# VectorE's share of a softmax exponential: the closing sum made of 16-bit tiles, a second GpSimd pass, and a new port rule and pace table in the instruction plan

## The chip, the cores and the metric

One core of one Trainium2 chip runs the whole program. The core has TensorE (PE in the profile; its weight loads are PEld), VectorE (DVE), ScalarE (ACT), GpSimd (POOL) and SyncE (SP), which here issues the DMAs. The metric is the device time of one execution in microseconds; the kernel before took 835.02 us (median of 3 runs, 834.14 to 835.98).

## The reference

```
x = x + A(layernorm(x)); x = x + B(layernorm(x))      # twice, same weights
A: qkv = x @ wqkv; 16 heads of 28; p = softmax(q k^T * 28**-0.5); (p v) @ wo
B: relu(x @ w1 + b1)**2 @ w2 + b2
```

x has 2048 rows of 448 in bf16, B's hidden width is 1792. In each of the two layers the softmax takes the exponential of 16 x 2048 x 2048 scores; the rest is matrix products, two layernorms and a squared relu.

## The kernel before, in words

The scores of one layer are cut into units. A unit is 128 keys by 512 columns, as two or four key blocks of one head against 256 or 128 queries. There are 2048 units in the two layers. TensorE writes three units into one group of PSUM banks (`s_stream`, matmuls at L956); one ScalarE instruction takes the exponential of a whole group, 128 x 1536 (L986 in `e_stream`), and writes bf16 into a tile `pt`. TensorE then multiplies by the values (L1127 in `p_stream`).

Some units are taken from ScalarE and given to VectorE and GpSimd. Then the group's ScalarE instruction is 128 x 1024 wide, and the third unit is worked by four instructions (`a_unit` and `a_rest`), on scores that are already multiplied by 128 times log2(e):

- the **take**, VectorE, L1034: from PSUM into a 32-bit tile w (`v_w`, or spare room in `K_sb`), score plus a shift, held from below. The shift is such that the low 16 bits of the 32-bit float hold the fraction of the power of two;
- the **part**, GpSimd, L1051: the low 16 bits of w (read as uint16, every second one), minus a middle, times a factor, to a bf16 tile (`pt`'s third bank, `pd`, or spare room in `V_sb` and `h`);
- the **bend**, VectorE, L1057: that bf16 tile squared in place;
- the **close**, VectorE, L1064: one scalar-tensor-tensor, w plus a constant plus the bend, rounded to int16. Its 16 bits are the bf16 exponential.

The order of every instruction of every engine is written out when the program is built. A planner (`Planner.run`) keeps a clock per engine, takes an estimated duration for each piece of work (`Op`), and at each step issues the candidate that could start first, then the one of smaller priority number. Pieces with `port=True` are planned so that one of GpSimd and one of VectorE do not overlap: the later one is planned from the end of the other. All units are handed out in that run: `apart` gives a unit to VectorE only if a set w is free, if VectorE was not more than 99.5% planned in the last 11 us, and if its backlog (the planned clock less now, plus `left`, the estimate of work that opened units still owe) is not above an entry of the table PACE, which has 128 entries over the run. The order is fixed on the chip; what moves is only when the semaphores let an instruction go.

Around the exponentials the planner puts everything else: the projections (L686 with evictions L705, L709, L737), layernorm (L528, L533, L649 on VectorE, L555 and L556 on GpSimd), output sums (L1154, L1156), the normalisation by DMA through DRAM (L1231, L1236, L1242, L1250, L1255), the hidden layer (L1322, and the square L1331) and the residual sums (L1264). Before a group of scores, TensorE repeats its score matmuls when the plan has it idle there (`again`).

Of the kernel before, what the change touches and what calls it, by code (L numbers as in the profile page):

```python
# [11 lines left out]
DT = mybir.dt  # L12
AF = mybir.ActivationFunctionType
ALU = mybir.AluOpType
# [9 lines left out]


FRAC = 7
GY = 0.617
XL = 0.25
TICK = 1.8
# [1 line left out]
WARM2 = 0.55  # L31
SHARE = 0.9
YL = 0.05
GN = 0.718
GM = 1.275
GS = 1.3
# [8 lines left out]
EXP_BITS = (127.0 - 0.085177) * 128 - EXP_SHIFT  # L45
# [37 lines left out]
LEAD = 15  # L83
LAST = 690
BUSY = 0.995
PACE = (2.2, 2.2, 2.2, 2.2, 1.8, 2.2, 2.2, 1.4, 3.0, 1.4, 1.4, 1.4, 2.2, 3.2, 3.6, 2.2, 2.2, 2.2, 2.2, 2.2, 0.6, 3.4, 2.6, 1.8, 1.0, 1.8, 2.6, 2.6, 2.2, 3.8, 3.0, 2.2, 2.2, 3.6, 2.2, 0.6, 3.0, 1.8, 1.8, 1.8, 1.8, 2.6, 2.2, 2.2, 1.4, 3.4, 2.6, 1.0, 2.2, 3.4, 3.6, 3.6, 1.4, 2.2, 3.0, 2.6, 3.8, 3.4, 1.8, 1.0, 2.6, 2.6, 2.2, 2.2, 3.8, 3.0, 1.8, 1.0, 3.8, 3.0, 1.8, 2.2, 2.2, 1.4, 3.2, 4.4, 2.6, 3.6, 3.6, 1.4, 1.8, 3.6, 3.0, 3.0, 3.0, 3.0, 2.2, 2.2, 2.2, 2.2, 3.0, 3.0, 1.8, 2.2, 2.6, 2.6, 1.4, 1.4, 4.0, 3.6, 3.6, 1.8, 1.8, 2.2, 2.2, 3.6, 1.4, 1.4, 2.2, 4.0, 1.8, 1.4, 2.2, 1.8, 2.6, 2.6, 2.2, 2.2, 2.6, 2.2, 2.8, 3.2, 1.4, 1.8, 1.8, 2.2, 2.2, 2.2)
SPAN = 11
NPT = 11
NOS = 2
# [58 lines left out]
class Planner:  # L148
# [61 lines left out]
    def run(self):  # L210
        while self.streams:
            cands = []
            for st in self.streams:
                s, e = self.earliest(st[2]) if st[2] is not None else (None, None)
                if s is not None:
                    cands.append((s, st[0](s) if callable(st[0]) else st[0], e, st))
            assert cands, "no stream can go on"
            known = cands

            due = next((c[3][2].ready for c in cands if c[1] == 0), None)  # L220
            if due is None:
                due = next((c[0] + c[3][2].dur + LAT["ACT"] for c in cands if c[1] == 1), None)
            if due is not None:
                ok = [c for c in cands if c[2] != "PE" or c[1] == 0 or c[0] + c[3][2].dur <= due + self.slack()]
                cands = ok or cands
            s, _, e, st = min(cands, key=lambda c: (max(c[3][2].ready, self.clock[c[2]]) if c[2] == "PE" and self.turns() else c[0], c[1]))
            o = st[2]
            o.eng = (e,)
            if o.acq:
                o.res = min((r for r in (o.acq() if callable(o.acq) else o.acq) if r.when() is not None), key=lambda r: r.when())  # L230
                o.turn = len(o.res.rel)
                o.res.rel.append(None)
            o.start, o.end = s, s + o.dur
            if e == "PE":
                o.room = min([c[0] for c in known if c[2] == "PE" and c[3] is not st] or [1e9]) - o.end
            if o.fn:
                o.fn(e)
            o.end += o.more
            self.clock[e] = o.end - (OVER if e == "DVE" and o.dur > 0.1 else 0.0)
            if e == "PE":  # L240
                self.mode = o.mode
            if o.port and e in self.ports:
                self.ports[e] = [*self.ports[e][-5:], (s, o.end)]
            if e == "PE" and o.end > s:
                self.used = [u for u in self.used if u[1] > s - 2 * TICK] + [(s, o.end, SHARE * o.dur if o.w is None else o.w)]
            if e in self.past:
                self.past[e] = [p for p in self.past[e] if p[1] > s - 40.0] + [(s, max(s, self.clock[e]))]
            for a in o.rel:
                a.got.append(o.end + o.lat + LAT[e])
                if len(a.got) == a.need:  # L250
                    a.res.rel[a.turn] = max(a.got)
            for key in o.sets:
                self.tok[key] = o
            st[2] = next(st[1], None)
            if st[2] is None:
                self.streams.remove(st)
# [3 lines left out]
def kernel(  # L260
# [12 lines left out]
    nc = tc.nc  # L273
    _, S, D = A_x.shape
# [6 lines left out]

    q_scale = float(DH) ** -0.5 * float(np.log2(np.e)) * 2.0 ** FRAC

# [255 lines left out]
    def layernorm(t0, nt, deps_of, early=False, mv=None, place=None, x_in=None, parts=False):  # L539
# [95 lines left out]
        for p0 in range(0, nt, wide):  # L635
# [4 lines left out]
            for j in js:  # L640
# [11 lines left out]
                on = NORMG and not early  # L652
                nm = Op("POOL" if on else "DVE", GN if on else 0.39, norm, deps=[rss[j], *([] if x_in is None else [x_in])], sets=[("n", t0, j)] if early else (), port=True)
                yield nm
# [181 lines left out]
    left = [0.0]  # L836

    def sets_of(unit):

        pi, kb, r, hh = unit  # L840
        l, qb, *_ = passes[pi]
        if l == 0:
            return R_v if 2 <= qb <= 6 else R_v[:4]
        return R_v

    def apart(i, now, us, soon=SOON):
# [22 lines left out]
        if pl.load(SPAN, "DVE") > BUSY:  # L869
            return None  # L870
        if max(0.0, pl.clock["DVE"] - now) + left[0] > PACE[i * len(PACE) // len(units)]:
            return None
# [93 lines left out]
    def apart_from(gi, t):  # L966

        if "read" in gbuf[gi]:
            tc.declare_no_dep(t.ins, gbuf[gi]["read"].ins, reason="both read the scores, in banks of their own")
        gbuf[gi]["read"] = t  # L970

    def e_stream():
        gi = 0
        while gi < len(gbuf) or s_left:
# [8 lines left out]
            def fn(e, gi=gi, n=n):  # L983
                e_now[:] = [e_now[0] + n // 512 + ("x" in gbuf[gi]), gi]
                pt = gbuf[gi]["pt"]
                t = nc.scalar.activation(out=pt[:, 0:n], in_=gbuf[gi]["sc"][:, 0:n], func=AF.Exp,  # L986
                                         scale=float(np.log(2.0)) * 2.0 ** -FRAC)
                if gbuf[gi].get("x") is gbuf[gi]["s"]:
# [17 lines left out]
    def pd_of(o):  # L1006
        i = R_pd.index(o.res)
        if i == 0:
            return vp.tile([P, 512], DT.bfloat16, name="pd")[:, :]
        if i < 5:  # L1010
            return V_sb[1][:, 11 + i, :, :].rearrange("p h r -> p (h r)")
        if i > 5:
            return V_sb[0][:, 8 + i, :, :].rearrange("p h r -> p (h r)")
        return hp.tile([P, QB], DT.bfloat16, name="h")[:, :]

    v_w = [const.tile([P, 512], DT.float32, name=f"v_w{k}") for k in range(4)]
    two = lambda a: a.rearrange("p (a n) -> p a n", a=2)

    def set_of(res, l):

        k = R_v.index(res)
        if k < 4:
            return two(v_w[k][:, :])
        keys = K_sb[1 - l][:, :, S - 512:S] if l == 0 else K_sb[0][:, :, 0:512]
        return keys[:, 2 * k - 8:2 * k - 6, :].bitcast(DT.float32)

    def a_unit(gi, x, src, unit, l):
        yield Op("-", 0.0, None, deps=[("s", gi)])
        box = {}

        def take(e):
            pending[0] -= 1
            box["w"] = set_of(c.res, l)
            t = nc.vector.tensor_scalar(out=box["w"], in0=two(src), scalar1=EXP_SHIFT,  # L1034
                                        scalar2=EXP_LOW, op0=ALU.add, op1=ALU.max)
            if x is gbuf[gi]["s"]:
                apart_from(gi, t)
        c = Op("DVE", 0.69, take, deps=[("s", gi)], acq=sets_of(unit), rel=x)
        left[0] += 1.54
        yield c  # L1040
        left[0] -= 0.6
        pl.spawn(lambda now: V_LAST if e_now[1] - gi >= V_AGE or at[0] > ends_at[unit[0]] + V_PAST else V_LATE if now > c.end + V_WAIT else V_PRIO if gi > FIRST else V_FIRST, a_rest(gi, c, box, unit))

    def a_rest(gi, c, box, unit):

        own = gbuf[gi]["in"]

        def part(e):
            pd = gbuf[gi]["pd"] = gbuf[gi]["pt"][:, 1024:1536] if own else pd_of(y)
            low = box["w"].bitcast(DT.uint16).rearrange("p a (n t) -> p a n t", t=2)[:, :, :, 0]  # L1050
            nc.gpsimd.tensor_scalar(out=two(pd), in0=low, scalar1=-EXP_MID * 65536, scalar2=EXP_BEND, op0=ALU.add, op1=ALU.mult)  # L1051
        y = Op("POOL", GY, part, deps=[c, ("p", gi)] if own else [c], acq=None if own else lambda: pd_free(unit), port=True, lat=YL)
        yield y

        def bend(e):
            pd = gbuf[gi]["pd"]
            nc.vector.tensor_tensor(out=pd, in0=pd, in1=pd, op=ALU.mult)  # L1057
        h = Op("DVE", 0.42, bend, deps=[y], port=True)
        yield h
        left[0] -= 0.34  # L1060

        def close(e):
            pd = gbuf[gi]["pd"]
            nc.vector.scalar_tensor_tensor(out=two(pd.bitcast(DT.int16)), in0=box["w"], scalar=EXP_BITS, in1=two(pd),  # L1064
                                           op0=ALU.add, op1=ALU.add)
        o = Op("DVE", 0.683, close, deps=[h], rel=c, sets=("x", gi), port=True, lat=XL)
        gbuf[gi]["x"] = y
        yield o
        left[0] -= 0.6

    norm_done = {}
    rows_done = set()
# [531 lines left out]
```

## Time and profile before

| | before |
|---|---|
| median of 3 runs | 835.02 us |
| span of the profiled execution | 834.4 us |
| instructions in it | 26688 |
| ScalarE busy | 815.2 us |
| VectorE busy | 793.5 us |
| TensorE busy (modelled) | 780.0 us |
| GpSimd busy | 234.8 us |
| units on VectorE (takes, L1034) | 272 |

The span runs from the first to the last instruction; here it is 0.6 us below the median of the runs. Busy is the union of an engine's instruction records, so time in which an instruction's record is open but waits inside for a port counts as busy. Records of neighbouring VectorE instructions overlap a little, so the spacing of two starts is what one costs, and not its own length.

### The profile page before, as it was taken

What the parts mean: (1) busy time and instruction counts of PE and PEld (TensorE: products, weight loads), DVE (VectorE), ACT (ScalarE), POOL (GpSimd) and SP (SyncE); (2) the same over time, 40 slices, a digit from 0 to 9 for tenths busy, and PEclk for the clock granted to TensorE, in tenths of its full rate; (3) what the DMA queues carried; (4) which work ended last, traced back from release to release, by engine and by line L of the source; (5) the groups of instructions that cost most, each with busy time, mean ns of one, the idle gap of its engine ahead of it and who ended that gap; (6) DMA issues with size and microseconds to landing.
All of it is one profiled execution on the core that took longest, in us unless ns stands there. A gap on an engine that the chain in (4) does not pass through costs nothing.

```text
span 834.4 us, 26688 instructions
## 1 busy us (share of the span) xinstructions
PE 780.0 (93%) x11403; PEld 405.6 (49%) x11403; DVE 793.5 (95%) x1646; ACT 815.2 (98%) x700; POOL 234.8 (28%) x366
## 2 busy tenths in 40 slices
PE   8999889999999999998999999989999999999997
PEld 4445545554444455444444544435454544545565
DVE  7999999999999999999999999999999999999955
ACT  8999999999999999999999999999999999999993
POOL 3222232233223232322223223332223132242200
PEclk9999999999999999999999999699999999999999
DMA  9200100000000000000000000011000000000000
GB/s 247 75 2 3 28 16 15 15 15 16 15 3 14 15 15 16 15 5 12 2 2 2 2 2 3 16 29 29 24 18 20 20 26 21 21 16 12 21 14 13
DMA packets 32359, 17.88 MB, mean 21 GB/s; under 512 B 17833, under 2 KB 31787, under 8 KB 32240
## 3 DMA queue, kind: packets, MB, share of 16 engines
q1 hardware_dynamic: 32240, 16.18, 7.0%
q8 instruction: 89, 1.46, 0.7%
q14 instruction: 30, 0.25, 0.1%
HBM read 13.88 MB, written 2.07 MB: 19 GB/s over the span
## 4 chain that ended last, share of the span: by engine, by line
DVE 40%; ACT 26%; PE 25%; issue 8%; DMA 0%; POOL 0%; ACTq 0%; DVEq 0%
ACT pt L986 26%; PE mt L686 10%; PE sc L956 8%; DVE v_w L1034 6%; DVE pt L1064 5%; PE oT L1127 4%; DVE r L1322 4%; DVE pt L1057 3%; DVE K_sb L1034 3%; DVE V_sb L1064 2%; DVE x_sb L1264 2%; DVE V_sb L1331 1%; DVE h L1064 1%; DVE V_sb L1057 1%; DVE xn L649 1%
## 5 line engine op out<-in xcount | busy, mean ns | idle before, releaser
L986 ACT ACTIVATE pt<-sc 128x1536 bf16<-128x1536 f32 (+1 forms) x683 | 803.8, 1407 | 4.3 <-PE sc L956 3.3
L956 PE MATMUL sc<-Q_sb,K_sb 32*128 32x256 bf16 (+1 forms) x4412 | 278.4, 267 | 36.0 <-ACT pt L986 28.6
L956 PEld LDWEIGHTS <-K_sb 32*128 32x128 bf16 x4412 | 106.6, 92 | 213.3 <-issue 154.7
L1127 PE MATMUL oT<-pt,V_sb 128*32 128x256 bf16 (+1 forms) x4004 | 154.8, 270 | 1.1 <-DVE K_sb L596 0.4
L1034 DVE TENSOR_SCALAR v_w<-sc 128x512 f32<-128x512 f32 x194 | 131.2, 681 | 4.1 <-PE sc L956 3.3
L686 PE MATMUL mt<-xnT,w 128*128 128x256 bf16 (+1 forms) x872 | 116.4, 272 | 3.6 <-DVE r L1322 0.9
L1127 PEld LDWEIGHTS <-V_sb 128*32 128x32 bf16 x4352 | 91.8, 96 | 53.8 <-issue 47.9
L1051 POOL TENSOR_SCALAR pt<-v_w 128x512 bf16<-128x512 uint16 x85 | 61.4, 723 | 158.6 <-DVE v_w L1034 138.5
L686 PEld LDWEIGHTS <-w 128*128 128x128 bf16 x896 | 75.8, 98 | 37.2 <-issue 28.2
L1322 DVE TENSOR_SCALAR r<-mt 128x512 bf16<-128x512 f32 x107 | 72.5, 680 | 2.6 <-PE mt L686 2.3
L1051 POOL TENSOR_SCALAR V_sb<-v_w 128x512 bf16<-128x512 uint16 x54 | 39.2, 726 | 101.6 <-DVE v_w L1034 101.4
L686 PE MATMUL mt<-w,V_sb 128*128 128x448 bf16 x260 | 66.9, 355 | 0.0
L1064 DVE SCALAR_TENSOR_TENSOR pt<-v_w,pt 128x512 int16<-128x512 f32 x85 | 57.2, 680 | 0.0
L1034 DVE TENSOR_SCALAR K_sb<-sc 128x512 f32<-128x512 f32 x78 | 52.9, 680 | 2.4 <-PE sc L956 1.9
L1057 DVE TENSOR_TENSOR pt<-pt 128x512 bf16<-128x512 bf16 x109 | 49.1, 463 | 0.0
L1264 DVE TENSOR_TENSOR x_sb<-x_sb,mt 128x448 bf16<-128x448 bf16 x61 | 37.1, 609 | 5.5 <-PE mt L686 5.3
L1057 DVE TENSOR_TENSOR V_sb<-V_sb 128x512 bf16<-128x512 bf16 x89 | 40.1, 460 | 0.0
L528 DVE BATCH_NORM_STATS2 st<-x_sb 128x6 f32<-128x448 bf16 x63 | 38.6, 614 | 1.6 <-DMA x_sb<-in_A_x_dram 1.2
L1051 POOL TENSOR_SCALAR V_sb<-K_sb 128x512 bf16<-128x512 uint16 x35 | 24.6, 703 | 51.7 <-DVE K_sb L1034 44.3
L1064 DVE SCALAR_TENSOR_TENSOR V_sb<-v_w,V_sb 128x512 int16<-128x512 f32 x54 | 37.5, 694 | 0.1
L686 PEld LDWEIGHTS <-V_sb 128*128 128x128 bf16 x302 | 24.5, 98 | 25.7 <-issue 12.6
L1051 POOL TENSOR_SCALAR h<-v_w 128x512 bf16<-128x512 uint16 x29 | 20.5, 708 | 45.1 <-DVE v_w L1034 44.3
(141 smaller groups left out, 911.1 us busy)
## 6 DMA issues: line engine op xcount, KB each, us to landing
rec<-scr SPq DMA_DIRECT2D x54, 128.0 KB
x_sb<-in_A_x_dram SPq DMA_DIRECT2D x8, 224.0 KB
out_dram<-x_sb SPq DMA_DIRECT2D x15, 112.0 KB
w<-in_B_w_dram SPq DMA_DIRECT2D x1, 1568.0 KB
w<-in_B_w_dram SPq DMA_DIRECT2D x1, 1344.0 KB
dn<-oT_sb SPq DMA_DIRECT2D x54, 4.0 KB
V_sb<-in_A_wqkv_dram SPq DMA_DIRECT2D x4, 168.0 KB
scr<-dn SPq DMA_DIRECT2D x27, 8.0 KB
```

The source lines that it names most:

```text
L528: nc.vector.bn_stats(out=box["st"][:, :], in_=x_sb[:, t0 + j, :] if src is None else src())
L649: nc.vector.tensor_scalar(out=xn[:, 0:D], in0=x_sb[:, t0 + j, :], scalar1=mv[0][:, j, 0:1], scalar2=ln[j], op0=ALU.subtract, op1=ALU.mult)
L686: nc.tensor.matmul(box["t"][:, c0:c0 + n], lhsT=lhsT() if callable(lhsT) else lhsT, rhs=rhs, start=a, stop=b)
L956: nc.tensor.matmul(dst[k][:, i * nt * P:(i + 1) * nt * P], lhsT=K_sb[l][rows, g, (kb + i) * P:(kb + i + 1) * P], rhs=Q_sb[rows, g, t0 * P: ...
L986: t = nc.scalar.activation(out=pt[:, 0:n], in_=gbuf[gi]["sc"][:, 0:n], func=AF.Exp, scale=float(np.log(2.0)) * 2.0 ** -FRAC)
L1034: t = nc.vector.tensor_scalar(out=box["w"], in0=two(src), scalar1=EXP_SHIFT, scalar2=EXP_LOW, op0=ALU.add, op1=ALU.max)
L1051: nc.gpsimd.tensor_scalar(out=two(pd), in0=low, scalar1=-EXP_MID * 65536, scalar2=EXP_BEND, op0=ALU.add, op1=ALU.mult)
L1057: nc.vector.tensor_tensor(out=pd, in0=pd, in1=pd, op=ALU.mult)
L1064: nc.vector.scalar_tensor_tensor(out=two(pd.bitcast(DT.int16)), in0=box["w"], scalar=EXP_BITS, in1=two(pd), op0=ALU.add, op1=ALU.add)
L1127: nc.tensor.matmul(box["t"][DHP * hh:DHP * hh + DHP, 0:n], lhsT=V_sb[l][:, kb + i, 4 * g + hh, :], rhs=p[:, c0:c0 + n], start=begin and kb ...
L1264: nc.vector.tensor_tensor(out=x_sb[:, tb, lo:hi], in0=x_sb[:, tb, lo:hi], in1=t[:, 0:hi - lo], op=ALU.add)
L1322: nc.vector.tensor_scalar(out=r[:, 0:w], in0=t[:, 0:w], scalar1=0.0, scalar2=None, op0=ALU.max)
```

## The change

After the part, GpSimd runs a second pass over w (`whole`): all 512 32-bit scores plus the constant, rounded to int16, written in place into the first half of w. The close becomes a tensor-tensor sum of two 16-bit tiles: the bend, and the int16 scores. The planner is told the new costs (1.28 instead of 1.54 for a unit; 0.617 for the second pass), gets a rule that puts a GpSimd candidate 0.6 us back when a VectorE candidate with `port` could start within 0.7 us of it and no other VectorE candidate could, and a new PACE table.

```
+PENB = 0.6
+PW = 0.7
+GZ = 0.617
...
-PACE = (2.2, 2.2, 2.2, 2.2, 1.8, 2.2, 2.2, 1.4, 3.0, ...
+PACE = (1.8, 1.8, 1.8, 1.8, 1.8, 1.8, 1.8, 1.8, 1.8, ...
...
+            free = min((c[0] for c in known if c[2] == "DVE" and not c[3][2].port and c[3][2].dur > 0.2), default=1e9)
+            locked = min((c[0] for c in known if c[2] == "DVE" and c[3][2].port), default=1e9)
+            def key(c):
+                if c[2] == "PE" and self.turns():
+                    return max(c[3][2].ready, self.clock[c[2]]), c[1]
+                k = c[0]
+                if c[2] == "POOL" and locked < c[0] + PW and free > c[0] + PW:
+                    k += PENB
+                return k, c[1]
+            s, _, e, st = min(cands, key=key)
...
-        left[0] += 1.54
+        left[0] += 1.28
...
+        def whole(e):
+            box["t"] = box["w"][:, 0, :].bitcast(DT.int16)
+            nc.gpsimd.tensor_scalar(out=two(box["t"]), in0=box["w"], scalar1=EXP_BITS, scalar2=1.0, op0=ALU.add, op1=ALU.mult)
+        z = Op("POOL", GZ, whole, deps=[y], port=True, lat=YL)
+
         def bend(e):
             pd = gbuf[gi]["pd"]
             nc.vector.tensor_tensor(out=pd, in0=pd, in1=pd, op=ALU.mult)
         h = Op("DVE", 0.42, bend, deps=[y], port=True)
+
+        def close(e):
+            pd = gbuf[gi]["pd"]
+            nc.vector.tensor_tensor(out=pd.bitcast(DT.int16), in0=pd, in1=box["t"], op=ALU.add)
+        o = Op("DVE", 0.42, close, deps=[h, z], rel=c, sets=("x", gi), port=True, lat=XL)
+        gbuf[gi]["x"] = y
+        yield z
         yield h
...
-        def close(e):
-            pd = gbuf[gi]["pd"]
-            nc.vector.scalar_tensor_tensor(out=two(pd.bitcast(DT.int16)), in0=box["w"], scalar=EXP_BITS, in1=two(pd),
-                                           op0=ALU.add, op1=ALU.add)
-        o = Op("DVE", 0.683, close, deps=[h], rel=c, sets=("x", gi), port=True, lat=XL)
...
-        left[0] -= 0.6
+        left[0] -= 0.34
```

The new PACE table is 1.8 in nearly all of its 128 entries; some twenty differ (0.6 to 4.4). The old one ran from 0.6 to 4.4 with 2.2 the commonest. Because the planner's costs, key and table differ, the whole order differs between the two programs, on every engine.

More of the change, by code (lines that the diff above doesn't have):

```diff
@@ L85 @@
 BUSY = 0.995
-PACE = (2.2, 2.2, 2.2, 2.2, 1.8, 2.2, 2.2, 1.4, 3.0, 1.4, 1.4, 1.4, 2.2, 3.2, 3.6, 2.2, 2.2, 2.2, 2.2, 2.2, 0.6, 3.4, 2.6, 1.8, 1.0, 1.8, 2.6, 2.6, 2.2, 3.8, 3.0, 2.2, 2.2, 3.6, 2.2, 0.6, 3.0, 1.8, 1.8, 1.8, 1.8, 2.6, 2.2, 2.2, 1.4, 3.4, 2.6, 1.0, 2.2, 3.4, 3.6, 3.6, 1.4, 2.2, 3.0, 2.6, 3.8, 3.4, 1.8, 1.0, 2.6, 2.6, 2.2, 2.2, 3.8, 3.0, 1.8, 1.0, 3.8, 3.0, 1.8, 2.2, 2.2, 1.4, 3.2, 4.4, 2.6, 3.6, 3.6, 1.4, 1.8, 3.6, 3.0, 3.0, 3.0, 3.0, 2.2, 2.2, 2.2, 2.2, 3.0, 3.0, 1.8, 2.2, 2.6, 2.6, 1.4, 1.4, 4.0, 3.6, 3.6, 1.8, 1.8, 2.2, 2.2, 3.6, 1.4, 1.4, 2.2, 4.0, 1.8, 1.4, 2.2, 1.8, 2.6, 2.6, 2.2, 2.2, 2.6, 2.2, 2.8, 3.2, 1.4, 1.8, 1.8, 2.2, 2.2, 2.2)
+PACE = (1.8, 1.8, 1.8, 1.8, 1.8, 1.8, 1.8, 1.8, 1.8, 1.8, 1.4, 1.8, 1.8, 1.8, 1.8, 1.8, 1.8, 1.8, 1.8, 1.8, 1.8, 1.8, 1.0, 1.4, 1.0, 1.8, 1.8, 1.8, 1.8, 1.8, 1.8, 1.8, 1.8, 1.8, 1.8, 1.8, 1.8, 1.8, 1.8, 1.8, 1.8, 1.8, 1.8, 1.8, 1.8, 1.8, 1.8, 1.8, 1.8, 1.8, 1.8, 1.8, 1.8, 1.8, 1.8, 1.8, 1.8, 1.8, 1.8, 1.8, 1.8, 1.8, 1.8, 1.8, 1.8, 1.8, 1.8, 1.8, 1.8, 1.8, 1.8, 1.8, 1.8, 1.8, 1.8, 1.8, 1.8, 1.8, 1.4, 1.6, 1.8, 1.8, 1.8, 1.8, 1.8, 1.8, 3.8, 2.6, 3.0, 3.4, 1.8, 0.6, 1.6, 4.4, 1.8, 1.8, 1.8, 2.6, 1.8, 1.8, 1.8, 1.8, 1.8, 1.8, 1.8, 1.8, 1.8, 1.8, 1.8, 1.8, 1.8, 1.8, 1.8, 1.8, 1.8, 1.8, 1.4, 1.8, 1.8, 1.8, 1.8, 1.8, 1.8, 1.8, 1.8, 1.8, 1.8, 1.8)
 SPAN = 11
@@ L225, in run @@
                 cands = ok or cands
-            s, _, e, st = min(cands, key=lambda c: (max(c[3][2].ready, self.clock[c[2]]) if c[2] == "PE" and self.turns() else c[0], c[1]))
+            free = min((c[0] for c in known if c[2] == "DVE" and not c[3][2].port and c[3][2].dur > 0.2), default=1e9)
[8 more added lines that the diff above has]
+            s, _, e, st = min(cands, key=key)
             o = st[2]
@@ L1058, in a_rest @@
         h = Op("DVE", 0.42, bend, deps=[y], port=True)
+        def close(e):
[4 more added lines that the diff above has]
+        yield z
         yield h
         left[0] -= 0.34
-        def close(e):
-            pd = gbuf[gi]["pd"]
-            nc.vector.scalar_tensor_tensor(out=two(pd.bitcast(DT.int16)), in0=box["w"], scalar=EXP_BITS, in1=two(pd),
-                                           op0=ALU.add, op1=ALU.add)
-        o = Op("DVE", 0.683, close, deps=[h], rel=c, sets=("x", gi), port=True, lat=XL)
-        gbuf[gi]["x"] = y
         yield o
-        left[0] -= 0.6
+        left[0] -= 0.34
     norm_done = {}
```

## Prediction

> **What bounds the kernel now.** I began with the head of the page and its busy times, then split the span into its opening, the stream of exponentials and the end (windows view; columns: length, PE, PEld, DVE, ACT, POOL busy with counts, clock, DMA share, GB/s).
>
> ```profile
> PE 780.0 (93%) x11403; PEld 405.6 (49%) x11403; DVE 793.5 (95%) x1646; ACT 815.2 (98%) x700; POOL 234.8 (28%) x366
> DVE 40%; ACT 26%; PE 25%; issue 8%; DMA 0%; POOL 0%; ACTq 0%; DVEq 0%
> ```
>
> ```profile
> 0.00:10.90 10.90, 8.67 (x55) 4.84 (x55) 6.75 (x29) 8.24 (x12) 5.49 (x15) 1.00 0.78 205
> 10.90:50.00 39.10, 37.10 (x494) 19.50 (x490) 37.09 (x88) 38.99 (x31) 10.42 (x21) 1.00 0.41 115
> 50.00:780.00 730.00, 686.13 (x9809) 348.65 (x9811) 714.30 (x1439) 726.42 (x623) 214.37 (x324) 0.99 0.05 14
> 780.00:818.30 38.30, 36.20 (x925) 23.99 (x914) 27.52 (x67) 38.30 (x31) 3.97 (x7) 1.00 0.06 16
> 818.30:834.40 16.10, 11.92 (x144) 8.59 (x142) 7.89 (x27) 3.21 (x7) 0.56 (x1) 1.00 0.05 15
> ```
>
> From 10.9 to 818.3 us ScalarE hardly rests: in the 730 us of the middle it idles 730 - 726.4 = 3.6 us. VectorE idles 15.7 us there (97.85% busy) and TensorE 43.9. The chain of waits crosses all three, so any of them could be next, but the one without slack is ScalarE. The waits say the same: TensorE waits for ScalarE, hardly the other way round.
>
> ```profile
> PE sc L956 <- ACT pt L986: 28.6, 69, 0.9
> ACT pt L986 <- PE sc L956: 3.3, 9, 0.6
> ```
>
> So the question is how many exponentials leave ScalarE, and whether VectorE, with GpSimd beside it, can really carry them.
>
> **The change part by part.** The instruction lists of the two programs, compared engine by engine, give the counts. Takes, bends and closes go from 272 to 305 each. ScalarE keeps 683 exponentials, but 410 wide and 273 narrow ones become 377 and 306: 33 units move. GpSimd has 305 parts and 305 second passes instead of 272 parts.
>
> *ScalarE.* Both widths stand in the lines view by form:
>
> ```profile
> L986 ACT ACTIVATE pt<-sc 128x1536 bf16<-128x1536 f32 x410 | 592.5, 1577 | 2.8 <-PE sc L956 2.2 <-PE oT L1127 0.2
> L986 ACT ACTIVATE pt<-sc 128x1024 bf16<-128x1024 f32 x273 | 291.7, 1152 | 1.5 <-PE sc L956 1.2
> ```
>
> The records overlap each other, but the startup is in both, so their difference is what 512 columns cost: 1577 - 1152 = 425 ns. 33 x 0.425 = **14.0 us** leave the engine that has no slack. The takes are spread evenly over both instruction lists, so nothing piles up at an end.
>
> *VectorE.* What an instruction costs is the spacing of starts in a stretch without waits:
>
> ```profile
> 219.76 0.41 DVE L1057 TENSOR_TENSOR pd<-pd 128x512 bf16<-128x512 bf16 x1
> 220.10 0.41 DVE L1331 TENSOR_TENSOR h<-r 128x512 bf16<-128x512 bf16 x1
> 220.43 0.68 DVE L596 COPY xnT<-tp 128x1024 bf16<-128x1024 bf16 x1
> 221.03 0.68 DVE L1034 TENSOR_SCALAR K_sb<-sc 128x512 f32<-128x512 f32 x1
> 221.63 0.68 DVE L1064 SCALAR_TENSOR_TENSOR pd<-v_w,pd 128x512 int16<-128x512 f32 x1
> 222.23 0.24 DVE L1236 RECIPROCAL dn<-dn 128x16 f32<-128x16 f32 x1
> ```
>
> A bend costs 0.34, a take 0.60, the old close 0.60. The new close has no row: int16 beside bf16 is not summed anywhere here. Its ends are the bend's 0.34 (two 16-bit inputs, same size) and the old close's 0.60 (int16 out); I take 0.34, the row with the same operation and widths. A unit then costs 0.60 + 0.34 + 0.34 = 1.28 instead of 1.54, and VectorE's units 305 x 1.28 - 272 x 1.54 = 390.4 - 418.9 = **-28.5 us**; 262 of 272 takes lie in the middle window, so about -27.4 there. (VectorE: DVE Perf Modes of the Trainium skill, section What auto-detection actually checks, gives the doubled rate when every tensor is 16-bit with step one, which would be 0.34; no run here shows it for int16.)
>
> *GpSimd, and the port.* The second pass has no row either. Nearest is the part, also 512 elements per partition read four bytes apart, 16 bits out, two ALU operations:
>
> ```profile
> L1051 POOL TENSOR_SCALAR V_sb<-v_w x54: 619/620/1093, 31.8 to 739.2; 128x512 bf16<-128x512 uint16 x54
> L730 POOL MEMSET V_sb<- 128x64 bf16 x16 | 2.3, 153 | 0.7
> 155.68 1.32 POOL L1051 TENSOR_SCALAR pt<-v_w 128x512 bf16<-128x512 uint16 x2 [0.28 <-DVE v_w L1034]
> ```
>
> I take the part's 0.62 (two of them back to back: 1.32, so 0.70 each); the ends are the memset's 0.15 and the longest part's 1.09. By itself the pass costs nothing, because GpSimd idles 72% of the span. What it costs is this:
>
> ```profile
> 229.81 0.67 DVE L1064 SCALAR_TENSOR_TENSOR V_sb<-v_w,V_sb 128x512 int16<-128x512 f32 x1
> 230.05 0.93 POOL L1051 TENSOR_SCALAR pt<-v_w 128x512 bf16<-128x512 uint16 x1 [3.10 <-DVE v_w L1034]
> 230.41 0.83 DVE L1057 TENSOR_TENSOR V_sb<-V_sb 128x512 bf16<-128x512 bf16 x1
> 231.16 0.41 DVE L1154 COPY oT_sb<-oT 128x256 f32<-128x256 f32 x1
> ```
>
> ```profile
> L1034 DVE TENSOR_SCALAR v_w<-sc x194: 646/681/694, 29.4 to 790.7; 128x512 f32<-128x512 f32 x194
> ```
>
> A part that starts inside a close takes 0.93 instead of 0.62, and the bend that starts inside that part takes 0.83 instead of 0.41. The take, which reads PSUM, never shows this: its longest is 694 ns. SBUF — State Buffer of the Trainium skill, section Who interferes with whom, states it as a lock: a VectorE instruction with two SBUF inputs and a GpSimd instruction that reads SBUF exclude each other for a whole instruction; the rows agree. By that rule the new close still takes the port, and the second pass takes it once more per unit, so it speaks against this change; what it can cost is the first rival.
>
> ```profile
> L1057 DVE TENSOR_TENSOR pt<-pt x109: 354/414/834, 121.3 to 765.5; 128x512 bf16<-128x512 bf16 x109
> L1057 DVE TENSOR_TENSOR pt<-pt 128x512 bf16<-128x512 bf16 x109 | 49.1, 463 | 0.0
> L1057 DVE TENSOR_TENSOR h<-h 128x512 bf16<-128x512 bf16 x38 | 17.1, 455 | 0.0
> L649 DVE TENSOR_SCALAR xn<-x_sb,mv,rstd x63: 303/390/776, 5.3 to 801.5; 128x448 bf16<-128x448 bf16 x63
> L649 DVE TENSOR_SCALAR xn<-x_sb,mv,rstd 128x448 bf16<-128x448 bf16 x63 | 27.6, 461 | 1.2 <-POOL rstd L556 0.7 <-PE mt L1552 0.5
> L1331 DVE TENSOR_TENSOR V_sb<-r x67: 361/416/829, 135.5 to 815.2; 128x512 bf16<-128x512 bf16 x67
> L1331 DVE TENSOR_TENSOR V_sb<-r 128x512 bf16<-128x512 bf16 x67 | 29.2, 440 | 0.5
> L1064 DVE SCALAR_TENSOR_TENSOR pt<-v_w,pt x85: 620/679/1100, 123.4 to 766.6; 128x512 int16<-128x512 f32 x85
> 0.00:834.40 834.40, 187.66 (x272) 0.99 0.08 21
> ```
>
> The last row is all closes (windows of line L1064): 690 ns each. Mean less median is what blocking costs VectorE now: bends 272 x (0.46 - 0.414) = 12.5, layernorm 63 x 0.07 = 4.5, squares 67 x 0.024 = 1.6, closes 272 x 0.01 = 2.7, together about 21 us. In the middle window parts are busy 187.65 us (windows of line L1051), 25.7%:
>
> ```profile
> 50.00:780.00 730.00, 187.65 (x262) 0.99 0.05 14
> ```
>
> Afterwards it is 2 x 305/272 x 187.65 = 420.8 of 716 us, 58.8%, 2.29 times; VectorE's port instructions grow from 714 to 780 (two per unit, 107 squares, 63 norms), 1.09 times. If blocking grows in proportion, it becomes 21 x 2.29 x 1.09 = 52.5: **31.5 more**. If the planned turns keep it where it is, **0 more**. I take half, **+16**. For the low side: the order keeps the two apart on paper for their full length, while the blocked bend above ended 0.27 after its part, less than its own 0.34. For the high side: 255 of 305 second passes stand directly behind their part, exactly when the bend becomes ready.
>
> VectorE in the middle: 714.3 - 27.4 + 16 = 702.9 of 716, 98.2% against 97.85%. It stays just under.
>
> *The rest.* New wait: the close needs the second pass too, and a stalled close holds every take behind it, whose PSUM bank TensorE then lacks. But on average 8.4 VectorE instructions stand between a take and its bend (8.6 before), some 4.2 us at 714.3/1439 = 0.50, and part plus pass need 1.4; I cost it at nothing while that cover holds. TensorE repeats 42 more score matmuls (4454 against 4412), 42 x 278.4/4412 = 2.6 us:
>
> ```profile
> L956 PE MATMUL sc<-Q_sb,K_sb 32*128 32x256 bf16 (+1 forms) x4412 | 278.4, 267 | 36.0 <-ACT pt L986 28.6
> ```
>
> They are planned into its idle time. SP issues the same DMAs; one denominator fetch moves behind a neighbour, the five bias-sum DMAs ahead of one normalisation, some stores past others; with a DMA share of 0.05 I cost that at nothing. The port rule and PACE issue no instruction; they act through the counts above.
>
> *Sum.* Span 834.4 - 14.0 = 820.4. Part comes back: TensorE's idle time shrinks from 43.9 to 716 - 686.1 - 2.6 = 27.3 us, so I let ScalarE's 3.6 us of gaps grow by the same ratio, to 5.8: +2.2. Span 822.6; the median lies 0.6 above the span, so **823.2 us**.
>
> **The rivals.**
>
> 1. *The port eats it; slower.* Place: bends and closes behind part and pass. With blocking in full proportion VectorE needs 714.3 - 27.4 + 31.5 = 718.4 us; at its present 97.85% that is a middle of 734.2 instead of 730: 839.2 us. The point of decision: 27.4 us more blocking uses up the saving, and VectorE sets 835 again. For it: VectorE at 97.85% and 255 passes behind their parts; against it: the turns, and 8.4 instructions of cover.
> 2. *The change doesn't do what it says: the new close runs at 0.60, or the pass is long.* At 0.60 VectorE's units cost 305 x 1.54 = 469.7, +50.8, 48.9 of it in the middle: 714.3 + 48.9 + 16 = 779 us, at 97.85% a middle of 796 and about 901 us. At 1.09 a pass, GpSimd's units fill 210 + 294 x 1.09 = 531 of 716 us, 74%, and blocking in proportion is 66, +45: 732 us, a middle of 748, about 853 us. For it only that both lack rows.
> 3. *TensorE becomes the bound.* Then 688.7 us must fit. Its best share of the middle is unknown beyond 94%; at 95.5% the middle is 721, 5 us above 716: 826 us, still faster. Against it: 28.6 us of its idle time was waiting for ScalarE.
>
> **How the numbers follow.** Forecast 0.56 (818 to 829); TensorE 0.13; port 0.25, of which blocking near the point of decision gives 0.07 within 0.2%; the two missing rows 0.06. A measurement here can tell about 0.2% from no change, that is 833.4 to 836.7. Faster 0.56 + 0.13 = 0.69, same 0.07, slower 0.18 + 0.06 = 0.24. The range starts where ScalarE loses even its gaps (820.4 - 3.6 + 0.6 = 817.4) and reaches past the port's 839.2 to 841; outside stay the missing rows and a worse port.
>
> **What would show it.** Right: 683 exponentials with ScalarE still over 99% in its stream, the second pass near 620, the close near 414, VectorE's blocking under 48 us. Wrong: bends or closes with means above 500 ns; ScalarE idle on score matmuls that wait for a take; a new close with a median of 680; the take waiting on nothing but VectorE's own queue while ScalarE pauses.

## The result, and the profile after

The changed kernel takes 880.2 us (median of 4 runs, 877.99 to 887.23) against 835.33 us before: ratio 1.0549, 95% interval 1.0504 to 1.0595. The forecast was 823.2 us. The profiled execution has a span of 885.5 us, so it is the slowest of the four (887.23); read differences of a few us in it with that in mind.

The page after, its busy times and its chain of waits:

```profile
PE 798.9 (90%) x11435; PEld 402.4 (45%) x11435; DVE 836.4 (94%) x1746; ACT 816.3 (92%) x699; POOL 453.7 (51%) x704
DVE 66%; PE 20%; issue 8%; POOL 3%; ACT 2%; DMA 0%; DVEq 0%; ACTq 0%; POOLq 0%
```

VectorE was to lose 28.5 us of work, less some blocking; it gained 42.9. Its share of the chain that ended last goes from 40% to 66%, ScalarE's from 26% to 2%. The waits (engine, line, what for: us in total, times, longest) show how that reaches the end:

```profile
PEld L968 <- DVE v_w L1046: 53.6, 95, 1.8
ACT pt L998 <- PE sc L968: 44.4, 93, 1.9
PE sc L968 <- DVE v_w L1046: 20.5, 38, 1.3
PE sc L968 <- ACT pt L998: 12.1, 30, 0.9
```

TensorE now waits for takes, because a take that comes late holds the PSUM bank of the next scores; and ScalarE waits 44.4 us for those scores, where it had waited 3.3. The wait the other way round, TensorE for ScalarE, has shrunk from 28.6 to 12.1.

The instructions themselves have the lengths that were taken for them. The source view gives shortest, median and longest in ns of the second pass and of the new close:

```profile
L1069 POOL TENSOR_SCALAR v_w<-v_w x217: 619/666/1186, 32.9 to 839.6; 128x512 int16<-128x512 f32 x109
L1079 DVE TENSOR_TENSOR pt<-pt,v_w x82: 355/412/827, 132.2 to 815.6; 128x512 int16<-128x512 bf16 x82
L1079 DVE TENSOR_TENSOR V_sb<-V_sb,v_w x76: 354/415/829, 38.9 to 835.4; 128x512 int16<-128x512 bf16 x76
```

The shortest pass is 619, as the part's, and its median 666; the median close is 412 to 415, as the bend's. But the longest close is twice its median. Six rows of the timeline show why (start, length in us):

```profile
631.27 0.62 POOL L1069 TENSOR_SCALAR K_sb<-K_sb 128x512 int16<-128x512 f32 x1
631.57 0.60 DVE L1079 TENSOR_TENSOR pd<-pd,K_sb 128x512 int16<-128x512 bf16 x1
631.97 0.67 POOL L1063 TENSOR_SCALAR pt<-v_w 128x512 bf16<-128x512 uint16 x1
632.09 0.83 DVE L1074 TENSOR_TENSOR pt<-pt 128x512 bf16<-128x512 bf16 x1
632.72 0.67 POOL L1069 TENSOR_SCALAR v_w<-v_w 128x512 int16<-128x512 f32 x1
632.83 0.68 DVE L1046 TENSOR_SCALAR v_w<-sc 128x512 f32<-128x512 f32 x1
```

GpSimd runs pass, part, pass without a break. The close at 631.57 starts in the pass and ends 0.28 after it; the bend at 632.09 starts in the part and ends 0.28 after that. Only the take, at 632.83, runs its 0.68 beside the next pass undisturbed; the longest of all takes here is 0.69. All bends and all closes of the execution (windows of one line: length, busy and count, clock, DMA):

```profile
0.00:885.50 885.50, 171.28 (x305) 0.97 0.07 20
0.00:885.50 885.50, 148.94 (x305) 0.97 0.07 20
```

A bend occupies 562 ns on average, a close 488 (busy time of the window over the count, so overlaps of neighbouring records count once). The experiments give the lengths without blocking, in the same order: 396 and 404 ns.

### The profile page after: what moved, and what is told of

It is laid out like the page before. It is cut to its first block, busy times and chain, and to the rows that moved or that the text cites. A ratio compares the mean times of both kernels' runs of the same rounds, so it can differ in the third digit from the quotient of the medians.

```text
span 885.5 us, 27409 instructions
## 1 busy us (share of the span) xinstructions
PE 798.9 (90%) x11435; PEld 402.4 (45%) x11435; DVE 836.4 (94%) x1746; ACT 816.3 (92%) x699; POOL 453.7 (51%) x704
## 4 chain that ended last, share of the span: by engine, by line
DVE 66%; PE 20%; issue 8%; POOL 3%; ACT 2%; DMA 0%; DVEq 0%; ACTq 0%; POOLq 0%
DVE v_w L1046 10%; PE mt L698 8%; PE sc L968 6%; DVE r L1339 6%; DVE pt L1074 5%; DVE pt L1079 5%; DVE K_sb L1046 4%; DVE V_sb L1074 4%; DVE V_sb L1079 3%; DVE x_sb L1281 3%; PE oT L1144 3%; DVE st L540 3%; DVE xn L661 3%; ACT pt L998 2%; DVE V_sb L1348 2%
## 5 line engine op out<-in xcount | busy, mean ns | idle before, releaser
L998 ACT ACTIVATE pt<-sc 128x1536 bf16<-128x1536 f32 (+1 forms) x683 | 805.6, 1282 | 53.5 <-PE sc L968 44.4
L1069 POOL TENSOR_SCALAR v_w<-v_w 128x512 int16<-128x512 f32 x217 | 148.9, 686 | 17.8
L1046 DVE TENSOR_SCALAR v_w<-sc 128x512 f32<-128x512 f32 x217 | 146.2, 677 | 7.1 <-PE sc L968 6.8
L1063 POOL TENSOR_SCALAR V_sb<-v_w 128x512 bf16<-128x512 uint16 x76 | 50.1, 659 | 66.2 <-DVE v_w L1046 63.0
L1074 DVE TENSOR_TENSOR pt<-pt 128x512 bf16<-128x512 bf16 x128 | 71.9, 573 | 0.5 <-POOL pt L1063 0.5
L698 PE MATMUL mt<-w,V_sb 128*128 128x448 bf16 (+1 forms) x288 | 70.5, 348 | 0.0
L1069 POOL TENSOR_SCALAR K_sb<-K_sb 128x512 int16<-128x512 f32 x88 | 60.6, 688 | 8.8 <-DVE K_sb L1348 1.6
L1063 POOL TENSOR_SCALAR pt<-K_sb 128x512 bf16<-128x512 uint16 x46 | 31.6, 686 | 48.1 <-DVE K_sb L1046 39.7
L1074 DVE TENSOR_TENSOR V_sb<-V_sb 128x512 bf16<-128x512 bf16 x96 | 54.2, 572 | 0.5 <-POOL V_sb L1063 0.5
L1079 DVE TENSOR_TENSOR pt<-pt,v_w 128x512 int16<-128x512 bf16 x82 | 40.7, 498 | 1.0
L1079 DVE TENSOR_TENSOR V_sb<-V_sb,v_w 128x512 int16<-128x512 bf16 x76 | 38.6, 513 | 0.6
```

Of the source, the lines that this page charges most:

```text
L698: nc.tensor.matmul(box["t"][:, c0:c0 + n], lhsT=lhsT() if callable(lhsT) else lhsT, rhs=rhs, start=a, stop=b)
L1069: nc.gpsimd.tensor_scalar(out=two(box["t"]), in0=box["w"], scalar1=EXP_BITS, scalar2=1.0, op0=ALU.add, op1=ALU.mult)
L1079: nc.vector.tensor_tensor(out=pd.bitcast(DT.int16), in0=pd, in1=box["t"], op=ALU.add)
```

## The experiments

Theory after the result, **port**: a VectorE instruction with two inputs in SBUF, begun while GpSimd reads SBUF, waits inside until GpSimd is done; the second pass doubles these meetings, and the waiting holds the takes behind it. Rivals: **GpSimd's time** (the pass makes results late), and **order** (33 more units, the new table and the new rule). In the table, blocked is what bends and closes occupy above their unblocked length (windows by line). That length is 0.396 and 0.404 us a piece, from the changed order without reads; for before and for the lower table it comes from their own order without reads. The three zeros are these references: no bend in them is longer than 0.428 us. The expectations count 23 us more in the changed kernel (99 instead of 76), because they include layernorms, squares and the multiplications of outputs.

| run | units | median us | ratio to before (95%) | DVE busy us | blocked us |
|---|---|---|---|---|---|
| before (profiled alone) | 272 | 835.0 | | 793.5 | 18 |
| changed | 305 | 880.2 | 1.0504 to 1.0595 | 836.4 | 76 |
| pass only writes | 305 | 834.65 | 0.9962 to 1.0001 | 785.3 | 37 |
| no pass | 305 | 832.72 | 0.9953 to 0.9989 | 786.5 | 40 |
| half pass | 305 | 848.06 | 1.0139 to 1.0178 | 801.3 | 50 |
| part and pass only write | 305 | 825.01 | 0.9847 to 0.9902 | 753.4 | 0 |
| lower table | 271 | 855.87 | 1.0214 to 1.0271 | 776.8 | 51 |
| lower table, only writes | 271 | 837.38 | 1.0000 to 1.0039 | 721.6 | 0 |
| before, only writes | 272 | 833.18 | 0.9950 to 0.9981 | 778.7 | 0 |

**The pass only writes.** The order of all instructions is that of the changed kernel.

```
-            nc.gpsimd.tensor_scalar(out=two(box["t"]), in0=box["w"], scalar1=EXP_BITS, scalar2=1.0, op0=ALU.add, op1=ALU.mult)
+            nc.gpsimd.memset(box["t"], 0)
```

> The changed kernel, same order of every instruction, but the second GpSimd pass only writes its 16-bit tile (a memset of 512 elements, about 0.53 us by the memset rows 153 ns for 64 and 205 ns for 128 elements) and reads nothing; the scores are left out of the sum. Port theory (bends, closes, norms and squares wait inside for a GpSimd instruction that reads SBUF; the chain of takes then waits for VectorE): blocking falls from about 99 us to between 26 and 48 us, VectorE's busy time from 836 to about 770 to 785, ScalarE fills its stream again, time 820 to 835. Rival 'the pass is simply more GpSimd time and its results come late': GpSimd is nearly as busy, so time stays above 865. Rival 'the new order and 33 more units are at fault': above 865 too.

834.65 us; VectorE busy 785.3. Its bends, then its closes:

```profile
0.00:832.70 832.70, 144.52 (x305) 1.00 0.08 22
0.00:832.70 832.70, 136.77 (x305) 1.00 0.08 22
```

45.5 us of the loss go with the reading of the second pass alone, while GpSimd still spends 0.52 us on each pass. Order and number of units alone, as a rival, are out: this is that order, with the same 305 units.

**No pass.** The close adds the bend to itself.

```
-            nc.gpsimd.tensor_scalar(out=two(box["t"]), in0=box["w"], scalar1=EXP_BITS, scalar2=1.0, op0=ALU.add, op1=ALU.mult)
...
-            nc.vector.tensor_tensor(out=pd.bitcast(DT.int16), in0=pd, in1=box["t"], op=ALU.add)
+            nc.vector.tensor_tensor(out=pd, in0=pd, in1=pd, op=ALU.add)
```

> The changed kernel in the same order, with the second GpSimd pass left out and the close adding the bend to itself (same size and rate), so the scores are left out of the sum. Port theory: as the write-only pass, 820 to 833, within 6 us of it, because what costs is the reading and not GpSimd's time. Rival 'more GpSimd time, late results': 820 to 830 here, but at least 30 us below the write-only pass. Rival 'order and units': still above 865.

832.72 us, 1.9 us under the run above. GpSimd's time is out as a rival too: an engine busy 403 us or 247 us makes no difference worth the name, as long as the pass reads nothing. But both runs stop some 10 us short of the forecast, and bends and closes still lose 40 us, to the parts:

```profile
0.00:833.20 833.20, 147.18 (x305) 0.99 0.08 21
0.00:833.20 833.20, 137.07 (x305) 0.99 0.08 21
```

**Part and pass only write.** The same once more for the part, again in the changed kernel's order.

```
-            nc.gpsimd.tensor_scalar(out=two(pd), in0=low, scalar1=-EXP_MID * 65536, scalar2=EXP_BEND, op0=ALU.add, op1=ALU.mult)
+            nc.gpsimd.memset(pd, 0.0)
...
-            nc.gpsimd.tensor_scalar(out=two(box["t"]), in0=box["w"], scalar1=EXP_BITS, scalar2=1.0, op0=ALU.add, op1=ALU.mult)
+            nc.gpsimd.memset(box["t"], 0)
```

> The changed kernel in its own order, 305 units, but both GpSimd passes only write (memsets of 512 elements, about 0.53 us each), so the exponential's mantissa and scores of these units are left out. If the blocking of VectorE by GpSimd's reads is the whole difference to the forecast, blocked time falls from 99 us to under 15, VectorE's busy time to 740 to 755, and the 33 exponentials saved on ScalarE show: 816 to 825. Rival 'the new order itself cannot feed ScalarE': 829 to 835, as the run in which only the second pass does not read (834.65).

825.01 us: with no reads on GpSimd the change is 1.25% faster than before, 1.8 us from the forecast. Part of that nearness is luck: the forecast kept before's blocking and added 16 us, and this run has none on bends and closes. Against before without reads (833.18, below) the gain is 8 us. Not one bend is blocked any more (the longest is 421 ns in this group and 424 in any), and ScalarE waits little for scores. Source view, the two windows rows of bends and closes, and the wait:

```profile
L1074 DVE TENSOR_TENSOR pt<-pt x128: 360/416/421, 121.4 to 754.6; 128x512 bf16<-128x512 bf16 x128
```

```profile
0.00:823.10 823.10, 120.90 (x305) 0.99 0.08 22
0.00:823.10 823.10, 123.36 (x305) 0.99 0.08 22
```

```profile
ACT pt L998 <- PE sc L968: 5.9, 14, 0.8
```

120.90/305 and 123.36/305 are the 0.396 and 0.404 us used above. So GpSimd's reads are the difference between 825 and 880, but for two things that the edit changes beside them. A memset is shorter; the run without a pass puts that at 2 us at most for the second pass. And the part's memset no longer waits for its take, so its result is earlier; but VectorE waited only 2.0 us for parts in the changed kernel (its five waits stand in the part on why the prediction was wrong).

**Half a pass.**

```
-            nc.gpsimd.tensor_scalar(out=two(box["t"]), in0=box["w"], scalar1=EXP_BITS, scalar2=1.0, op0=ALU.add, op1=ALU.mult)
+            nc.gpsimd.tensor_scalar(out=box["t"][:, 0:256], in0=box["w"][:, 0, :], scalar1=EXP_BITS, scalar2=1.0, op0=ALU.add, op1=ALU.mult)
...
-            nc.vector.tensor_tensor(out=pd.bitcast(DT.int16), in0=pd, in1=box["t"], op=ALU.add)
+            nc.vector.tensor_tensor(out=two(pd.bitcast(DT.int16)), in0=two(pd), in1=box["t"][:, 0:256].unsqueeze(1).to_broadcast([P, 2, 256]), op=ALU.add)
```

> The changed kernel in its own order, the second pass over half of the elements (256 instead of 512; the close takes that half twice, so half of the scores are left out), about 0.35 to 0.41 us instead of 0.62. Port theory with blocking by time: blocked time halfway between 48 us (no pass) and 99 (whole pass), 65 to 80 us, time 850 to 864. Rival 'each GpSimd instruction blocks once, whatever its length': 870 to 880.

848.06 us, a little under the range, and far under the 870 to 880 of the rival that each GpSimd instruction blocks once, whatever its length. Bends and closes:

```profile
0.00:848.60 848.60, 156.42 (x305) 0.98 0.08 21
0.00:848.60 848.60, 137.85 (x305) 0.98 0.08 21
```

Blocked 50 us, between 40 and 76. One order thus has a curve: blocked 0, 37, 40, 50, 76 us gives 825, 835, 833, 848, 880. The first 40 us cost 8 to 10; the next 36 cost 47, more than one for one.

**The plan's part.** Three runs take the new table and the new rule apart.

```
e3_old_table: the changed operations with
-PACE = (1.8, 1.8, 1.8, 1.8, ...
+PACE = (2.2, 2.2, 2.2, 2.2, ...
-                if c[2] == "POOL" and locked < c[0] + PW and free > c[0] + PW:
-                    k += PENB
e6_rule_old_table: the first of these edits alone
e8_table_no_rule: the second alone
```

> The changed operations with the old PACE table and without the rule that puts a GpSimd candidate back; 298 units instead of 305 go to VectorE. Port theory: the second pass is still there, blocking stays near 95 us, time 865 to 890. Rival 'the new table and the rule are at fault': back to 825 to 840.

> The changed operations with the second pass, old table, new rule for GpSimd's turns; 312 units on VectorE. If the table is what the plan costs: near 865 (860 to 870), as the old table without the rule. If the rule is what costs: 875 to 885. If the rule does keep the turns apart on the chip: blocked time clearly under the 89 us of the old table without it, and below 860.

> The changed operations with the second pass, new table, no rule; 283 units on VectorE. If the table is what the plan costs: 873 to 885. If the rule is what costs: 860 to 868. Fewer units by themselves: ScalarE 22 x 0.425 = 9 us more than the changed kernel, VectorE 22 x about 1.5 = 33 us less, so where VectorE sets the end this could also fall to 850.

865.2 us (ratio 1.0323 to 1.0371), 896.25 (median of three, 1.0707 to 1.0765) and 861.05 (1.0282 to 1.0333). With the units handed out: 283 units 861, 298 units 865, 305 units 880, 312 units 896. Each of these runs has the second pass, and among these four the more units an order gives to VectorE, the later it ends; two orders further down (289 units 878, 301 units 883) do not keep to that. The rule adds 14 units under the old table and 22 under the new one, and the time rises by 31 and 19 us. It was meant to keep the turns apart, and under the new table it does not: without it bends and closes lose 159.44 + 140.06 - 283 x 0.80 = 73 us, 0.26 a unit, and with it 0.25. Whether it hurts through the number of units alone or through the order as well isn't separated.

**Old operations under table and rule.** The kernel before, with the new PACE and the new key of the planner.

```
-PACE = (2.2, 2.2, 2.2, 2.2, ...
+PACE = (1.8, 1.8, 1.8, 1.8, ...
+                if c[2] == "POOL" and locked < c[0] + PW and free > c[0] + PW:
+                    k += PENB
```

> The old operations (no second pass, close of 32-bit scores, costs 1.54) with the new PACE table and the new rule for GpSimd's turns; 271 units on VectorE. Port theory: blocking stays near 26 us, time 832 to 842, no more than 1% from before. Rival 'table and rule are at fault': 860 or more.

852.99 us (1.0139 to 1.0235), between the two expectations: the new plan costs even the old operations 17 us, at a nearly equal number of units. Both theories had this wrong. Bends and closes lose 27 us in this order instead of 18 (117.07 + 196.24 us, less 270 at before's lengths without reads); the rest of the 17 us has no cause shown.

**No pass, old table, no rule.**

```
the edit of the run without the pass, and both edits of e3_old_table
```

> No second pass (close adds the bend to itself, scores left out), old table, no rule: 298 units on VectorE, that is 26 fewer wide exponentials than before. If the two costs add (pass about 45 us, table with rule about 15), this is what the cheaper close is worth alone: 880 - 45 - 16 = 819, and from ScalarE alone 835.8 - 26 x 0.425 = 825; 815 to 827. Rival 'the cheaper close never had the gain, another engine takes over at once': 831 or more, as the run without the pass under the new table.

844.24 us (1.0090 to 1.0131), not 819. The costs of pass and plan do not add: without the pass the new table and rule are 11.5 us better than the old, with it 15 us worse. The new plan hands out 7 more units, which is 7 x 0.425 = 3.0 us of ScalarE's time; the rest is order. VectorE is less in the way here than in the run without the pass under the new table, where it held 48% of the chain; the chain shares and ScalarE's wait:

```profile
PE 37%; ACT 36%; DVE 17%; issue 8%; DMA 0%; POOL 0%; ACTq 0%; DVEq 0%
```

```profile
ACT pt L996 <- PE sc L966: 17.9, 26, 2.8
```

What makes one order of the same operations some 8 us better than another, although it blocks more (40 us against 26), stays open.

**Before's number of units.**

```
-        if max(0.0, pl.clock["DVE"] - now) + left[0] > PACE[i * len(PACE) // len(units)]:
+        if max(0.0, pl.clock["DVE"] - now) + left[0] > PACE[i * len(PACE) // len(units)] - 0.7:
```

> The changed kernel with every entry of its table 0.7 lower, so that 271 units go to VectorE (before: 272), second pass and rule as in the changed kernel. Rival 'too many units were handed out, with before's number it is harmless': VectorE's free work is 70 us under before's, blocking at 0.32 us a unit is 87 us, together below before's busy time, so 833 to 843. Theory 'each blocked VectorE instruction also holds up the takes behind it, so blocking costs even when VectorE is not full': 848 to 865.

855.87 us. This hits hardest at the forecast's way of counting: VectorE is busy 776.8 us of 853.5, 91%, far from full, and the run is still 20 us slower than before. The next run takes only the reads away from this order (both edits of the run in which part and pass only write).

> The changed kernel with the lower table (271 units, 855.9), both GpSimd passes as memsets that read nothing (mantissa and scores of these units are left out). If blocked VectorE instructions alone made that run slow, although VectorE was only 91% busy: 830 to 840, since ScalarE's work is that of before. If its order is worse by itself: 843 or more.

837.38 us. The page's busy line without reads, and ScalarE's wait with them and without (first kernel: 271 units; second: only writes):

```profile
PE 787.2 (94%) x11543; PEld 411.9 (49%) x11543; DVE 721.6 (86%) x1644; ACT 814.8 (98%) x699; POOL 307.3 (37%) x636
```

```profile
ACT pt L998 <- PE sc L968: 17.0, 30, 2.6
```

```profile
ACT pt L998 <- PE sc L968: 6.1, 12, 0.9
```

So 18.5 of the 20 us are blocking again, on an engine with time to spare. TensorE's wait for takes falls with ScalarE's wait (PEld for `v_w`: 19.8 us with the reads, 4.0 without). The windows rows, bends and closes of 271 units, then of the same with only writes:

```profile
0.00:853.50 853.50, 138.93 (x271) 0.99 0.08 21
0.00:853.50 853.50, 134.53 (x271) 0.99 0.08 21
```

```profile
0.00:835.30 835.30, 110.52 (x271) 0.99 0.08 21
0.00:835.30 835.30, 112.22 (x271) 0.99 0.08 21
```

273.5 - 222.7 = 51 us blocked cost 18.5.

**Before without reads.** The kernel before, its only GpSimd pass as a memset.

> The kernel before in its own order, its only GpSimd pass as a memset that reads nothing (mantissa of the bend left out). Blocking goes from about 26 us to under 8. ScalarE has no slack there, so if blocking costs only where it makes ScalarE wait, 830 to 835; if every blocked microsecond counts, 812 to 825.

833.18 us, 2.8 us below before. Bends and closes, in the kernel before (its bends alone; its closes stand in the prediction) and here:

```profile
0.00:834.40 834.40, 119.06 (x272) 0.99 0.08 21
```

```profile
0.00:832.00 832.00, 106.43 (x272) 0.99 0.08 21
0.00:832.00 832.00, 182.25 (x272) 0.99 0.08 21
```

119.06 + 187.66 - 106.43 - 182.25 = 18 us blocked, and they cost 2.8. Between this order and the changed one, both without reads, ScalarE's busy time falls from 814.0 to 800.4 us.

**Two ways to keep the turns.** Both start from the changed operations with the old table and without the rule (865.2).

```
e9_bend_first:
-        yield z
         yield h
         left[0] -= 0.34
+        yield z
e10_pitch:
-GY = 0.617
+GY = 0.70
-GZ = 0.617
+GZ = 0.70
```

> The changed operations with the old table and without the rule (865.2), but the second pass is planned after its own bend instead of before it; 301 units. If the second pass directly behind its part is what meets the bend: blocked bends fall from 43 us to under 30, time 845 to 857. If turns do not hold on the chip wherever the pass is planned: blocking stays at 80 to 95 us, 860 to 875.

> The changed operations with the old table and without the rule, and the plan's cost of both GpSimd passes 0.70 (their spacing back to back) instead of 0.617; 289 units. If the turns fail because the plan takes GpSimd's passes too short: blocking falls from 89 us to under 60, time 835 to 850. If not: blocking 80 to 90 us, and 9 units fewer than 298 give 855 to 868.

883.29 us (1.0536 to 1.0580) and 878.39 (1.0475 to 1.0526): both above every range given, and both worse than where they started. With the bend planned first, bends and closes (301 units) read

```profile
0.00:879.40 879.40, 173.17 (x301) 0.99 0.07 20
0.00:879.40 879.40, 152.55 (x301) 0.99 0.07 20
```

which is 85 us blocked, more than the 65 of the starting point (159.03 + 144.61 - 298 x 0.80). Planning the passes at their true spacing leaves blocking where it was, 66 us for 289 units, and ScalarE waits longer for scores:

```profile
ACT pt L996 <- PE sc L966: 38.2, 42, 5.4
```

So neither the place of the pass directly behind its part nor the 83 ns that the plan was short is the cause of the blocking. The second run also shows that blocked time does not fix the time from one order to the next: 65 and 66 us go with 865 and 878. In none of the orders with the whole second pass did bends and closes lose less than 0.19 us a unit (51/271); without it, it was 0.07 (before) to 0.13.

## Why the prediction was wrong, point by point

- **ScalarE, 14.0 us saved: right as a term.** Without reads its busy time is 13.6 us less in the changed order than in before's (800.4 against 814.0), and 8 of these reach the time (825.0 against 833.2), where the sum said 12 (14.0 less 2.2). In the changed kernel itself the saving does not show: ScalarE is busy 816.3 us there, against 815.2 before. Its records overlap less while it waits for scores, so their mean lengths fall (1474 and 1047 ns against 1577 and 1152) but the time that they cover does not.
- **The new close at 0.34, the pass at 0.62: right but for blocking.** Their rows above; the passes occupy 209.47/305 = 0.69 us on average. The second rival is out. (Its 1.09 was the longest part of one tile; the longest of all parts before took 1.58.)
- **VectorE's free work, -28.5 us: right in kind.** Without any reads VectorE is busy 753.4 us, and 778.7 in the kernel before without reads: 25.3 less.
- **The cover of 8.4 instructions: right for the wait that it was meant for.** VectorE waits for GpSimd's results next to never; the five such waits of the changed kernel add up to 3.8 us:

```profile
DVE xn L661 <- POOL rstd L568: 1.6, 3, 0.9
DVE h L1074 <- POOL h L1063: 1.0, 2, 0.5
DVE V_sb L1074 <- POOL V_sb L1063: 0.5, 1, 0.5
DVE pt L1074 <- POOL pt L1063: 0.5, 1, 0.5
DVE h L1079 <- POOL v_w L1069: 0.2, 1, 0.2
```

- **The blocking, "I take half, +16", with 31.5 as the upper end: this step failed.** Bends and closes alone lost 76 us instead of 18, and the bends' mean of 562 ns is over the 500 that was named as a sign of being wrong. Three smaller groups lost as well (lines view; norms, one group of the squares, outputs):

```profile
L661 DVE TENSOR_SCALAR xn<-x_sb,mv,rstd 128x448 bf16<-128x448 bf16 x63 | 32.0, 527 | 1.6 <-POOL rstd L568 1.6
L1348 DVE TENSOR_TENSOR V_sb<-r 128x512 bf16<-128x512 bf16 x67 | 32.8, 493 | 0.1
L1272 DVE TENSOR_TENSOR oTn<-oT_sb,rec 128x512 bf16<-128x512 f32 x27 | 22.6, 836 | 0.0
```

Against the means of before, 461, 440 and 693 ns, that is 63 x 0.066 + 67 x 0.053 + 27 x 0.143 = 11.6 us more; with the 58 of bends and closes 69.6. Put into the forecast's own formula: 714.3 - 27.4 + 69.6 = 756.5 us for VectorE, at 97.85% a middle of 773, and 878 us. Measured: 880.2. The mechanism was the first rival's; the term that failed was the blocking, taken at +16 with a bound of 31.5, where the rows give 69.6. The windows row of the middle of the changed kernel:

```profile
50.00:831.00 781.00, 705.99 (x9851) 345.81 (x9850) 755.56 (x1537) 730.54 (x625) 425.34 (x649) 0.97 0.05 13
```

VectorE's 755.6 us are what that sum gives, but they fill 781 us, 96.7% and not 97.85%. That 878 comes within 2 us of the median is therefore partly luck.

- **Why the bound was too low.** It scaled before's blocking by GpSimd's share of the time. Inside one order that works: without the pass 40 us, with it 76, 1.9 times for twice the passes. But it started from before's blocking, 21 us with layernorm and squares (15 of them for bends and closes, where the run without reads gives 18), and that belongs to before's order. The changed order with the parts alone already has 40 (305 units). The low rate of before was a property of that one order and did not carry over; the turns that the planner writes down did not keep it.
- **"It stays just under": wrong as a test.** Full or not full did not decide. At 271 units VectorE was 91% busy, and blocking still cost 18.5 us: a take behind a blocked bend is late for TensorE, and the scores then for ScalarE, as both waits in those two runs say. The prediction had named this path, a stalled close that holds every take behind it, and cost it at nothing while the cover held. But the cover only keeps VectorE from waiting for a result; it does nothing about waiting inside an instruction for the port. The saturation formula hit 878 here, but it would have given that run nothing.
- **The costs of the plan** (table, rule) were set at nothing beyond their counts. With the old operations they cost 17 us, for which the prediction had no term. That this cost is also in the changed kernel is not shown: its own order without reads takes 825.0.
- **The chances.** 0.25 on the port was too little, given that the row of the blocked bend, the lock that SBUF — State Buffer of the Trainium skill describes (section Who interferes with whom) and 255 of 305 passes behind their parts all stood on one side, and on the other only that the planner meant to avoid it.

No version here beats the kernel before with its full computation.

## What to carry to other kernels

Moving a pass to an engine that idled 72% of the time was not free here, because that engine shares a port with the busy one. Before such a move, count how often the two would use the port, and do not take the rate of meetings from one order alone: with one pass a unit it was 0.07 us in before's order and 0.13 in the changed one. An upper bound found by scaling one order is no bound. To price such a conflict cleanly, let the suspected instruction write without reading in the same order: here that one edit, in two runs, put 55 us of loss down to the reads, 45.5 to the second pass and 9.6 to the part.

## What the runs showed of the hardware that was not expected

A GpSimd instruction that only writes leaves two-input VectorE instructions alone and still blocks one kind: with both passes as memsets (median 524 ns for 512 16-bit elements), the 63 layernorm instructions, with one full SBUF input and a 16-bit output, took 507 ns on average against a median of 392, while no bend, close or square was held.

```profile
L661 DVE TENSOR_SCALAR xn<-x_sb,mv,rstd 128x448 bf16<-128x448 bf16 x63 | 30.8, 507 | 1.6 <-POOL rstd L568 1.6
L1348 DVE TENSOR_TENSOR V_sb<-r 128x512 bf16<-128x512 bf16 x67 | 27.6, 415 | 0.1
```

Three rows of that run's timeline show one of them (start, length in us): the norm starts inside a memset and ends only 0.13 after the next one.

```profile
254.17 0.52 POOL L1069 MEMSET v_w<- 128x512 int16 x1
254.52 0.76 DVE L661 TENSOR_SCALAR xn<-x_sb,mv,rstd 128x448 bf16<-128x448 bf16 x1
254.63 0.52 POOL L1063 MEMSET V_sb<- 128x512 bf16 x1
```

SBUF — State Buffer of the Trainium skill, section Who interferes with whom, draws just this line: two SBUF inputs contend only with a GpSimd instruction that reads, an instruction in a two-port mode with any. These rows agree, if the norm runs in such a mode, which no run here tests by itself.
